# Unread 32x32 turns and 256 unread 32x32 products behind the second attention unit

## The chip, the cores and the metric

The kernel runs on one core of one Trainium2 chip. The metric is the device time of one execution in microseconds, from a median of several runs. TensorE's instructions appear in the profile twice: PE is the matmul, PEld the load of its stationary operand.

## The reference

One transformer block for one sequence of 2048 tokens of width 1024, in float32. A layer norm feeds an attention with 32 heads of 32 that works on four segments of 512 tokens: causal softmax inside a segment, and between segments a running memory (a sum of products of keys and values and a sum of keys, read with a positive map of the queries and mixed with the softmax part by a gate per head). A second layer norm, applied twice, feeds an MLP of width 3584 with gelu.

```python
h = x + A(layernorm(x))      # A: q, k, v = x @ wq, x @ wk, x @ wv; 32 heads, 4 segments of 512
    p = softmax(q @ k.T * scale + mask); a_dot = p @ v
    a_mem = phi(q) @ M / (phi(q) @ z + 1e-6)
    o = g * a_mem + (1 - g) * a_dot        # g = sigmoid(beta), one per head
    M, z = M + phi(k).T @ v, z + sum(phi(k))
    return o @ wo
out = h + B(layernorm(h))    # B: gelu(layernorm(y) @ w1 + b1) @ w2 + b2
```

## The kernel before

The kernel takes the tokens in two halves of 1024. In each half the attention is cut into 16 units, a unit being four heads (a group g) of one segment, in the order of the table `ORDER`. A unit takes 24 steps of the main loop in `attention`: eight steps each for keys, queries and values (`kps`, `qps`, `vps`), every step three products of 512 columns (`mm3`, lines 127 to 129: high by high, low by high, high by low parts, in fp32r). After each step `close` runs whatever was put on that step by `at`: splits of weights, softmax products of the unit before (`qk1`, `qk2`, `av` at line 634, whose 16 f32 products use four tiles of 32 columns), the memory's products, copies. Beside units 0 and 1 a generator `ln1` normalizes and turns the second segment's tokens (transposes `pt`, line 161).

The whole loop is recorded under `in_order()`: each engine keeps its instructions in the order in which the code writes them. An instruction that waits therefore holds up all that stands behind it on its engine.

Behind the last step of unit 1, in the first half only, the loop calls `constants()`. It makes the gate (ScalarE exp and add, lines 78 and 79, VectorE's reciprocal, line 80, ScalarE's complement, line 81), turns b1 (`pb`, lines 83 and 84) and spreads the gate by GpSimd (line 87). Then unit 2 begins with its `kps`.

Memory is taken from rings of slots. PSUM's rings are "d" with three banks (`kps`, `qps`, `vps`, `pb` and others), "qk" and "pt" with two banks each, and "av" with one. In SBUF the ring "ln" has four slots of 128x1024 floats; from unit 1 on, each unit takes two of them for `kk` and `qq`, the split keys and queries that DMAs then spread to `ks` and `qs` (line 418). Whoever takes a slot waits until its last readers are done.

Of the kernel before, what the change touches and what calls it, by code (L numbers as in the profile page):

```python
# [10 lines left out]
F32 = mybir.dt.float32  # L11
# [6 lines left out]
P = 128  # L18
S = 2048
D = 1024  # L20
# [31 lines left out]
def build(tc, x, wq, wk, wv, wo, beta, w1, b1, w2, b2, out):  # L52
    nc = tc.nc
# [3 lines left out]
    psum = top.enter_context(tc.tile_pool(name="psum", bufs=1, space=PSUM))  # L57

    def ps_dense(name):
        return psum.tile([P, 512], F32, tag="d", name=name, bufs=3)  # L60
# [16 lines left out]
    def constants():  # L77
        behind(nc.scalar.activation(bb, bb, AF.Exp, scale=-1.0))
        nc.scalar.activation(bb, bb, AF.Identity, bias=1.0)
        behind(nc.vector.reciprocal(gate[:, 0, :], bb))  # L80
        nc.scalar.activation(gate[:, 1, :], gate[:, 0, :], AF.Identity, scale=-1.0, bias=1.0)
        pb = ps_dense("pb")
        behind(nc.tensor.transpose(pb[:, :FB], b1r, ident[:FB, :FB]))
        nc.scalar.copy(b1c, pb[:, :FB])
        for j in range(4):
            b = slice(32 * j, 32 * j + 32)
            nc.gpsimd.tensor_copy(gcol[b, :], gate[b, 1, :].rearrange("p (g j) -> p g j", j=4)[:, :, j])
# [34 lines left out]
    def behind(op):  # L122

        tc.add_manual_dep(op.ins, acts["last"][op.ins.engine].name, NOSYNC, reason="program order")
# [240 lines left out]
    def attention(half, first):  # L365
# [355 lines left out]
        for n in range(16):  # L721
# [52 lines left out]
            if n == 1:  # L774
                for _ in side:
                    pass
                side = None
                if first:
                    constants()
                acts.pop("last", None)  # L780
# [658 lines left out]
    lnp = tc.alloc_tile_pool(name="lnp", bufs=1)  # L1439
# [142 lines left out]
```

## Time and profile before

| | us |
|---|---|
| median of 2 runs | 2175.62 (2174.37 to 2176.87) |
| the profiled execution, its time | 2176.5 |
| its span, first to last instruction | 2174.8 |
| TensorE busy in the span | 2154.5 (99%) |
| VectorE busy | 1357.8 (62%) |
| ScalarE busy | 1100.5 (51%) |
| GpSimd busy | 950.1 (44%) |

In a row of the timeline stand the start in the span, how long it took, engine, line, operation, what it writes and reads, and in square brackets how long the engine had idled and what ended that. In a row of the groups stand count, busy time and mean ns of one, then the idle time before them. A row of the windows has the stretch, its length, busy time of PE, PEld, DVE, ACT and POOL, the granted TensorE clock, and DMA's share and GB/s. In a row of one line's instructions stand the shortest, median and longest duration in ns. A row with x4 joins four instructions, and its time runs from the first start to the last end.

### The profile page before, as it was taken

Reading aid. Unit: us, or ns where it says so; the run is one execution under the profiler, and the core shown is the slowest. Engines: PE = TensorE matmul, PEld = TensorE weight load, DVE = VectorE, ACT = ScalarE, POOL = GpSimd, SP = SyncE. Lnnn points to the kernel's source line nnn. Section 1 sums busy time; section 2 is a strip of 40 time slices with the busy share of each in tenths; the row PEclk is TensorE's granted clock in tenths of the full one; section 3 lists DMA queues with packets and bytes.
Section 4 is the critical chain, followed back from the end, with each engine's and each line's share of the span. In section 5 each row is a group of like instructions: output and inputs, shape, how many; then the busy total and the mean of one; then the engine's idle time right before and its main releaser. Section 6 shows DMA issues by size and latency. Waiting matters only on the chain.

```text
span 2174.8 us, 33225 instructions
## 1 busy us (share of the span) xinstructions
PE 2154.5 (99%) x10937; PEld 1750.0 (80%) x10937; DVE 1357.8 (62%) x2696; ACT 1100.5 (51%) x2433; POOL 950.1 (44%) x1206
## 2 busy tenths in 40 slices
PE   8999999999999999999999999999999999999999
PEld 6877777778888888877777778888888788888887
DVE  7766666655745656666667655745666665576753
ACT  5777777753543445777777753633343232322321
POOL 5533335461434434533335551534446544255340
PEclk9999999999999999999999999999999999999999
DMA  7444444664575555444444763576569865676762
GB/s 202 117 117 107 107 107 127 198 203 155 169 211 154 180 163 152 121 117 107 107 107 125 204 214 134 170 213 174 160 202 380 280 223 178 201 241 214 260 227 91
DMA packets 352405, 376.20 MB, mean 173 GB/s; under 512 B 27214, under 2 KB 244330, under 8 KB 352234
## 3 DMA queue, kind: packets, MB, share of 16 engines
q1 hardware_dynamic: 289306, 337.25, 51.3%
q10 hardware_dynamic: 62928, 36.84, 5.7%
q8 instruction: 87, 1.43, 0.3%
q14 instruction: 84, 0.69, 0.1%
HBM read 241.27 MB, written 82.38 MB: 149 GB/s over the span
## 4 chain that ended last, share of the span: by engine, by line
PE 95%; DVE 2%; ACT 1%; DMA 1%; POOL 1%; issue 0%; SPq 0%; ACTq 0%; DVEq 0%; POOLq 0%
PE po L1418 24%; PE bps L1021 11%; PE cps L1021 7%; PE dps L1021 7%; PE pst L620 4%; PE po L634 3%; PE pqk L570 3%; PE pwo L127 3%; PE vps L127 3%; PE pwo L129 3%; PE qps L127 3%; PE pwo L128 3%; PE kps L127 3%; PE qps L128 3%; PE qps L129 3%; PE vps L128 3%
## 5 line engine op out<-in xcount | busy, mean ns | idle before, releaser
L572 DVE CUSTOM_DVE_ANT_0 pqk<-pqk,mask 128x512 f32<-128x512 f32 (+2 forms) x384 | 216.9, 565 | 235.5 <-PE pqk L570 205.1
L574 ACT ACTIVATE junk<-pqk,mx 128x512 f32<-128x512 f32 (+2 forms) x384 | 225.1, 586 | 133.0 <-DVE mx L572 124.7
L627 POOL TENSOR_SCALAR_AFFINE_SELECT e<-e 128x128 f32<-128x128 f32 (+1 forms) x384 | 136.0, 357 | 259.0 <-ACT e L623 253.9
L700 POOL TENSOR_TENSOR wl<-wr,wh 128x256 fp32r<-128x256 f32 x268 | 200.6, 764 | 107.2 <-DVE wh L696 43.5
L623 ACT ACTIVATE e<-pst 128x384 f32<-128x384 f32 (+1 forms) x384 | 200.4, 528 | 67.4 <-PE pst L620 66.4
L1428 DVE TENSOR_TENSOR c<-c,po 128x512 f32<-128x512 f32 x160 | 105.4, 683 | 150.7 <-PE po L1418 143.4
L620 PE MATMUL pst<-qs,ks 104*128 104x512 f32 (+3 forms) x512 | 140.7, 318 | 2.2 <-ACT e L623 1.2
L570 PE MATMUL pqk<-ks,qs 96*128 96x512 f32 (+2 forms) x384 | 137.8, 359 | 0.9 <-ACT junk L574 0.6
L620 PEld LDWEIGHTS pst<-qs,ks 104*128 104x128 f32 x512 | 95.7, 188 | 36.1 <-ACT e L623 11.5
L1418 PE MATMUL po<-w2h,zh 128*128 128x512 f32 x378 | 121.0, 390 | 2.0 <-ACT zh L1357 1.6
L1275 POOL TENSOR_TENSOR w2r<-w2r 128x512 f32<-128x512 f32 x54 | 83.0, 1547 | 70.9 <-DMA w2r<-in_B_w 65.0
L127 PE MATMUL qps<-yh,wh 128*128 128x512 f32 x256 | 113.1, 442 | 0.0
L127 PE MATMUL kps<-yh,wh 128*128 128x512 f32 (+1 forms) x264 | 113.0, 428 | 0.0
L1021 PE MATMUL bps<-zh,sb 128*128 128x512 f32 x336 | 111.0, 391 | 0.0
L1021 PE MATMUL bps<-zh,sa 128*128 128x512 f32 x336 | 110.8, 390 | 0.0
L1134 POOL TENSOR_TENSOR s<-r 128x512 f32<-128x512 f32 x28 | 44.0, 1571 | 142.3 <-DVE sa L1150 84.8
L127 PE MATMUL vps<-yh,wh 128*128 128x512 f32 x256 | 105.0, 410 | 0.0
L1418 PE MATMUL po<-w2h,hl 128*128 128x512 f32 x322 | 103.1, 390 | 0.0
L128 PE MATMUL kps<-yl,wh 128*128 128x512 f32 (+1 forms) x264 | 102.4, 388 | 0.6 <-DVE yl L165 0.3
L129 PE MATMUL kps<-yh,wl 128*128 128x512 f32 (+1 forms) x264 | 101.8, 386 | 0.0
L128 PE MATMUL qps<-yl,wh 128*128 128x512 f32 x256 | 101.0, 395 | 0.0
L128 PE MATMUL vps<-yl,wh 128*128 128x512 f32 x256 | 100.9, 394 | 0.0
(271 smaller groups left out, 6206.7 us busy)
## 6 DMA issues: line engine op xcount, KB each, us to landing
hr<-h_dram SPq DMA_DIRECT2D x112, 448.0 KB, 5.5
w2r<-in_B_w SPq DMA_DIRECT2D x122, 256.0 KB, 4.6
r<-in_B_w SPq DMA_DIRECT2D x56, 512.0 KB, 4.3
ks<-kk SPq DMA_DIRECT2D x360, 64.0 KB, 2.0
qs<-qq SPq DMA_DIRECT2D x360, 64.0 KB, 2.0
h_dram<-ht ACTq DMA_DIRECT2D x83, 256.0 KB, 3.8
wx<-in_B_w SPq DMA_DIRECT2D x56, 256.0 KB, 3.7
o_dram<-side SPq DMA_DIRECT2D x52, 256.0 KB, 4.3
```

Source lines behind the costliest of these rows:

```text
L127: nc.tensor.matmul(ps, ah, bh, start=first, stop=False)
L128: nc.tensor.matmul(ps, ah, bl, start=False, stop=False)
L129: acts["mm"] = nc.tensor.matmul(ps, al, bh, start=False, stop=last)
L570: nc.tensor.matmul(ps, u["qs"][0:96, j, i * P:(i + 1) * P], u["ks"][0:96, j, 0:n], start=True, stop=True)
L572: nc.vector.tensor_tensor_reduce(out=ps, in0=ps, in1=mask[:, 512 - n:512], op0=ALU.add, op1=ALU.min, scale=-SCALE, scalar=3.0e38, accum_out=m)
L574: at(now[0] + 1, lambda: nc.scalar.activation(acts["junk"][:, :n], ps, AF.Exp, bias=m, scale=-1.0, accum_out=u["mx"][:, 1, i, j:j + 1]))
L620: nc.tensor.matmul(ps[:, o:o + 512 - P * jk], u["ks"][:, j, jk * P:(jk + 1) * P], u["qs"][:, j, jk * P:512], start=True, stop=True)
L623: nc.scalar.activation(e, ps[:, :w], AF.Exp, scale=SCALE)
L627: nc.gpsimd.affine_select(d, d, pattern=[[0, 2], [1, P]] if n == 2 else [[1, P]], compare_op=ALU.is_ge, fill=0.0, base=0, channel_multipli ...
L700: nc.gpsimd.tensor_tensor(l[:, c], wr[:, c], raw(h)[:, c], op=ALU.subtract)
L1021: nc.tensor.matmul(ps, x_[:, c, :], y_[:, c, :], start=first and c == 0 and n == 0, stop=last and c == 3 and n == 2, skip_group_check=True)
L1418: nc.tensor.matmul(ps, x_[:, k], y_[k], start=opens and k == 0 and i == 0, stop=closes and k == self.KP - 1 and i == 2, skip_group_check=True)
```

## The change

In `constants()`, between the gate and b1's transpose, come: two tiles `ta` and `tb` from the ring "ln"; a memset of `ta` to 0.5 by VectorE; two turns in 32x32 blocks from `ta` to all of `tb`, 512 columns each; two more of 384 columns each over part of `tb`; and 256 products by TensorE. Each product uses one 32x32 tile of the array: row strip a (partitions 32a to 32a + 31 of both operands) and column strip j, accumulating over 16 steps b in PSUM bank a at partitions 32j on. The columns fall with b: 128, 96, 64 and 32, four steps each. The four banks are two of the ring "d", one of "qk" and one of "pt". Four copies by ScalarE write the banks back to `tb`. Nothing reads `tb` after that.

```diff
@@ -79,6 +79,27 @@
         nc.scalar.activation(bb, bb, AF.Identity, bias=1.0)
         behind(nc.vector.reciprocal(gate[:, 0, :], bb))
         nc.scalar.activation(gate[:, 1, :], gate[:, 0, :], AF.Identity, scale=-1.0, bias=1.0)
+        raw_ = lnp.tile([P, D], F32, tag="ln", name="ta", bufs=4)
+        turned = lnp.tile([P, D], F32, tag="ln", name="tb", bufs=4)
+        behind(nc.vector.memset(raw_, 0.5))
+        for k in range(2):
+            nc.vector.transpose(turned.rearrange("p (b c) -> p b c", c=64)[:, :, 32 * k:32 * k + 32],
+                                raw_[:, 512 * k:512 * k + 512].rearrange("p (b c) -> p b c", c=32))
+        for k in range(2):
+            nc.vector.transpose(turned[:, 512 * k:512 * k + 384], raw_[:, 512 * k:512 * k + 384])
+        pz = [psum.tile([P, 512], F32, tag=t, name="pz", bufs=n) for t, n in (("d", 3), ("d", 3), ("qk", 2), ("pt", 2))]
+        moving = turned.rearrange("p (i x) -> p i x", i=4)
+        for b in range(16):
+            for a in range(4):
+                for j in range(4):
+                    n, rows_ = 4 - b // 4, slice(32 * a, 32 * a + 32)
+                    op = nc.tensor.matmul(pz[a][32 * j:32 * j + 32, 0:32 * n], raw_[rows_, 32 * b:32 * b + 32],
+                                          moving[rows_, 0:n, 32 * j:32 * j + 32], start=b == 0, stop=b == 15,
+                                          tile_position=(32 * a, 32 * j), skip_group_check=True)
+                    if b + a + j == 0:
+                        behind(op)
+        for a in range(4):
+            nc.scalar.copy(turned[:, 128 * a:128 * a + 128], pz[a][:, 0:128])
         pb = ps_dense("pb")
         behind(nc.tensor.transpose(pb[:, :FB], b1r, ident[:FB, :FB]))
         nc.scalar.copy(b1c, pb[:, :FB])
```

TensorE's order at that place, before: the last products of unit 1's values and the last four turns of tokens, the transpose of b1, then unit 2's keys.

```order
L128 MATMUL vps<-yl_205,wh 128x512
L129 MATMUL vps<-yh_204,wl 128x512
L161 MATMUL pt<-ident,xt 128x128 x4
L83 MATMUL pb<-ident,b1r 128x28
L127 MATMUL kps<-yh_485,wh 128x512
L128 MATMUL kps<-yl_486,wh 128x512
```

And now, with every line behind the insertion 21 higher:

```order
L150 MATMUL vps<-yh_204,wl 128x512
L182 MATMUL pt<-ident,xt 128x128 x4
L96 MATMUL pz<-tb,ta 32x128 x64
L96 MATMUL pz<-tb,ta 32x96 x64
L96 MATMUL pz<-tb,ta 32x64 x64
L96 MATMUL pz<-tb,ta 32x32 x64
L104 MATMUL pb<-ident,b1r 128x28
L148 MATMUL kps<-yh_485,wh 128x512
L149 MATMUL kps<-yl_486,wh 128x512
```

The 256 products stand ahead of b1's transpose and of all of unit 2's keys.

VectorE's order at that place now: the copy of the values, two low parts of turned tokens, the gate's reciprocal, then the new five, then the chain on `z` that ends in the row offsets `mh` of unit 0's second softmax pass.

```order
L517 COPY vt<-vps 128x512
L186 TENSOR_TENSOR yl_486<-pt,yh_485 128x4x128 x2
L80 RECIPROCAL gate<-bb 128x32
L84 MEMSET ta 128x1024
L86 STREAM_TRANSPOSE tb<-ta 128x16x32 x2
L89 STREAM_TRANSPOSE tb<-ta 128x384 x2
L619 TENSOR_TENSOR z<-z,mx 128x16
L620 SCALAR_TENSOR_TENSOR z<-z 128x16
```

Before, the reciprocal was followed by `z` at once; the memset and the four turns now stand between them. On ScalarE the four copies of `pz` (line 102) stand between the gate's complement (line 81) and the copy of b1.

## The prediction

> **What bounds the kernel now.** I read the page first: busy shares, then the chain that ended last.
>
> ```profile
> span 2174.8 us, 33225 instructions
> PE 2154.5 (99%) x10937; PEld 1750.0 (80%) x10937; DVE 1357.8 (62%) x2696; ACT 1100.5 (51%) x2433; POOL 950.1 (44%) x1206
> ...
> PE 95%; DVE 2%; ACT 1%; DMA 1%; POOL 1%; issue 0%; SPq 0%; ACTq 0%; DVEq 0%; POOLq 0%
> ```
>
> TensorE is busy 99% of the span and carries 95% of the chain. Time that it loses can come back only where it waits later. So the second view is its waits from 60 to 120 us, the stretch that begins where the change is put:
>
> ```profile
> PE kps L128 <- DVE yl L165: 0.3, 1, 0.3
> ```
>
> This is the only wait there: 0.3 us. What the change costs TensorE is therefore nearly all paid in the end. The third view is the timeline at that place.
>
> ```profile
> 60.16 0.60 PE L161 MATMUL pt<-ident,xt 128*128 128x128 f32 x4
> 60.36 0.69 DVE L496 COPY vt<-vps 128x512 f32<-128x512 f32 x1 [0.38 <-PE vps L129]
> ...
> 60.69 0.24 PE L83 MATMUL pb<-ident,b1r 28*128 28x28 f32 x1
> ...
> 60.86 0.50 PE L127 MATMUL kps<-yh,wh 128*128 128x512 f32 x1
> 60.97 1.51 DVE L165 TENSOR_TENSOR yl<-pt,yh 128x512 fp32r<-128x512 f32 x2
> ...
> 61.64 0.24 ACT L78 ACTIVATE bb<-bb 128x32 f32<-128x32 f32 x1
> ...
> 61.70 0.50 PE L128 MATMUL kps<-yl,wh 128*128 128x512 f32 x1 [0.34 <-DVE yl L165]
> ...
> 61.91 0.23 ACT L79 ACTIVATE bb<-bb 128x32 f32<-128x32 f32 x1
> ...
> 62.39 0.34 DVE L80 RECIPROCAL gate<-bb 128x32 f32<-128x32 f32 x1
> ...
> 62.65 0.11 DVE L598 TENSOR_TENSOR z<-z,mx 128x16 f32<-128x16 f32 x1
> ```
>
> TensorE reaches the constants at 60.69, two microseconds before VectorE has finished its own part of them at 62.39 + 0.34 = 62.73. The change puts VectorE's new instructions behind that reciprocal, and TensorE's products wait for them.
>
> **The change part by part.** *The wait.* The products read ta and tb, so TensorE stops at 60.69 until VectorE has done a memset of 128x1024, two turns of 128x512 and two of 128x384. No row shows a memset of this size or a turn; the nearest ones are
>
> ```profile
> L696 DVE CAST wh<-wr 128x1024 fp32r<-128x1024 f32 x66 | 46.3, 702 | 2.9 <-DMA wr<-in_A_wv 2.9
> L933 DVE TENSOR_TENSOR hb<-ht,b2c 128x1024 f32<-128x1024 f32 x16 | 19.2, 1209 | 1.8 <-DMA h_dram<-hb 1.3 <-DMA b2c<-in_B_b 0.5
> L496 DVE COPY vt<-vps 128x512 f32<-128x512 f32 x32 | 22.1, 691 | 0.4 <-PE vps L129 0.4
> L572 DVE CUSTOM_DVE_ANT_0 pqk<-pqk,mask 128x384 f32<-128x384 f32 x128 | 72.5, 566 | 100.8 <-PE pqk L570 98.4
> ```
>
> The memset lies between 0.70 (the cast) and 1.21 (the sum); I take 1.1. A turn of 512 columns lies between half of that cast, 0.35, and 0.69; I take 0.65, near the copy. One of 384 lies between 0.26 and 0.57; I take 0.50. Sum 1.1 + 1.3 + 1.0 = 3.4, and 0.1 for hand-overs between them (z at L598 follows the reciprocal without a gap). VectorE ends at 66.2 and TensorE starts at 66.3: **5.6 us** lost. From below the five cost 1.9 and the loss is 4.1. From above there is the same cast beside GpSimd:
>
> ```profile
> 54.25 6.74 POOL L700 TENSOR_TENSOR wl<-wr,wh 128x256 fp32r<-128x256 f32 x9
> ...
> 54.96 1.27 DVE L696 CAST wh<-wr 128x1024 fp32r<-128x1024 f32 x1
> ```
>
> 1.27 for 0.70; 1.8 times 3.4 is 6.2, a loss of 8.4. GpSimd's splits were done by 60.99, so I keep 5.6. Queued behind the waiting product stand the transpose of b1r and all of unit 2's projections; ScalarE's copies, VectorE's maxima and GpSimd's masks wait for those. Nothing of this runs ahead, so the pause hides nothing.
>
> *The products.* The 256 become 512 records if each makes two, as the head products at L634 do (1024 records for 32 units of 16). Those are four tiles of 32 columns side by side, and the nearest rows:
>
> ```profile
> 85.87 2.36 PE L634 MATMUL po<-e,vf 128*32 128x512 f32 x32
> 88.16 0.50 PE L127 MATMUL kps<-yh,wh 128*128 128x512 f32 x1
> 88.50 0.39 PE L128 MATMUL kps<-yl,wh 128*128 128x512 f32 x1
> ...
> 85.87 0.16 PEld L634 LDWEIGHTS po<-e,vf 128*32 128x32 f32 x8 [0.37 <-issue]
> ```
>
> ```profile
> L634 PEld LDWEIGHTS po<-e,vf x1024: 106/110/110, 85.9 to 1297.6; 128*32 128x32 f32 x171
> L634 PE MATMUL po<-e,vf x1024: 272/432/617, 85.9 to 1297.7; 128*32 128x512 f32 x43, 128*32 128x256 f32 x43, 128*32 128x128 f32 x43, 128*32 128x384 f32 x42
> ```
>
> A full-width transpose of 128 f32 columns takes (0.60 - 0.27)/3 = 0.11 us (four at 60.16, 0.27 being the record of one). One block at L634 streams 2 x 4 x (512 + 384 + 256 + 128) = 10240 columns, 8.8 us one after another; it took 88.16 - 85.87 = 2.29. So nearly four run abreast, each column strip on its own. The new products stream 2 x 64 x (128 + 96 + 64 + 32) = 40960 columns: 35.2 us one after another, 8.8 four abreast, 2.2 sixteen abreast. Row strips side by side occur nowhere in the trace. For starting them, eight loads of 0.11 in 0.16 us are (0.16 - 0.11)/7 = 7 ns apart, so 512 pairs need at least 512 x 7 ns = 3.6 us. Ends: 3.6 below, 56 above (512 x 0.11, each load's full time bare). I take **3.6**, sixteen abreast: what shares the array by columns so cleanly I expect to share it by rows, the four row strips writing four different banks.
>
> *The clock.* A pause of 5.6 us has no like between 14 us and the end. The ends of the trace show what one does:
>
> ```profile
> 8.23 1.97 PE L281 MATMUL pt<-ident,xt 128*128 128x128 f32 x8 [8.23 <-ACT xt L271]
> 10.54 3.85 PE L281 MATMUL pt<-ident,xt 128*128 128x128 f32 x16 [0.34 <-ACT xt L271]
> 14.15 0.37 PE L127 MATMUL kps<-yh,wh 128*128 128x256 f32 x1
> ```
>
> ```profile
> 2170.59 0.39 PE L1418 MATMUL po<-zh,hl 128*128 128x512 f32 x1
> ```
>
> ```profile
> 2164.00:2170.00 6.00, 6.00 (x28) 4.97 (x27) 0.69 (x1) 0.00 (x0) 0.00 (x0) 1.00 0.12 44
> 2174.00:2174.80 0.80, 0.00 (x0) 0.00 (x0) 0.00 (x0) 0.00 (x0) 0.00 (x0) 0.92 0.00 0
> ```
>
> After the last product's end at 2170.98 the granted clock (third column from the right) falls within the last 0.8 us, to a mean of 0.92: idle for under 3.8 us was enough. At the start, eight and then sixteen transposes take 1.97 and 3.85 us; 0.11 apart, as at 60.16, they would take 7 x 0.11 + 0.27 = 1.04 and 15 x 0.11 + 0.27 = 1.92. So half speed lasted from 8.23 to about 14, some 5.8 us. If that recurs, the first 5.8 us do 2.9 us of work: **+2.9**, from 0 (no drop) to about 5 (a longer one).
>
> The Trainium skill, "TensorE: Matmul & The Clock Gate", Part 1, has half rate after an idle window of about 3.4 us and full rate again after a busy window as long. The trace agrees on the fall (under 3.8 us), but its half speed lasted 5.8; by the page's window the term would be 1.7 and the sum 11.2.
>
> *Behind the products.* kps now takes the bank of the first pz and waits for ScalarE's copy of it.
>
> ```profile
> 62.91 0.17 ACT L84 COPY b1c<-pb 128x28 f32<-128x28 f32 x1
> ```
>
> ```profile
> L502 ACT COPY vf<-vn 128x512 f32<-128x512 f32 x32 | 18.8, 587 | 0.0
> ```
>
> 128 columns between 28 (0.17) and 512 (0.59) give 0.26. With 0.2 for the last record to end, 0.1 of signals and 0.1 for leaving the tiles (kps at 88.16 takes 0.34 to its successor, other 512-column products 0.23): **+0.65**, ends 0.4 and 1.5 (all four copies waited for). The 0.34 at 61.70 goes: yl is ready long before, **-0.35**, and no other wait is there to take its place.
>
> *At nothing.* ta and tb take two of the ring's four slots, so unit 2 writes kk where unit 1's still lay.
>
> ```profile
> 61.32 2.20 SPq L418 DMA_DIRECT2D ks<-kk  x3
> ...
> 63.58 2.00 SPq L418 DMA_DIRECT2D qs<-qq  x3
> ...
> 70.05 0.58 ACT L435 CAST kk<-kps 128x512 fp32r<-128x512 f32 x1
> ```
>
> Its last readers are issued by 65.6 and the write stood at 70.05, now 12 us later: covered by the pause itself. Without that cover it would be some 2 us. VectorE's z chain, 3.5 us late, feeds a TensorE step that stands behind the products: hidden by them.
>
> Sum: 5.6 + 3.6 + 2.9 + 0.65 - 0.35 = **12.4 us**. The profiled execution took 2176.5 (span 2174.8), 0.9 above the median 2175.62 and inside the runs' spread, so 2176.5 + 12.4 = **2189**, slower by 0.6%: inside the 2% that a measurement of this kernel can tell from no change.
>
> **Rivals.** *Four abreast.* Row strips take turns, only column strips overlap: 8.8 instead of 3.6, sum 17.6, **2194** (2199 if no pass of a tile takes less than 0.11: 128 turns of 0.11 = 14.1). For it: the trace has no row strips. Against: nothing but the likeness of rows to columns.
>
> *Strict order.* If a product's second pass must wait for its first on the same tile, and nothing overtakes it, only two passes ever overlap and each product adds one pass: 64 x 0.11 x (1 + 0.75 + 0.5 + 0.25) = 17.6 instead of 3.6, sum 26.4, **2203**. Against: the same rule gives L634 4 x 0.11 x (4 + 3 + 2 + 1) = 4.4 us where 2.29 was measured. For: sixteen tiles may exceed how far TensorE looks ahead; four do not. The Trainium skill, same page, Part 3 ("What overlaps and what doesn't") states such first-in-first-out order for products; the L634 row speaks against it here.
>
> *Nothing abreast.* Each small load costs its whole 0.11 before its product, 512 x 0.11 = 56 instead of 3.6: sum 65, **2241**, slower by 3%. It passes 2% once a record costs over some 69 ns: 43.5 us less the other 8.8 is 35, over 512. For it: with 32 columns little streaming covers a load, and the chip's instruction supply over 1024 dense ones isn't seen in the trace. Against: at L634 loads of 0.11 hid behind products that follow 0.11 apart.
>
> **How the numbers follow.** Forecast 0.58 (its own terms: 4.1 + 3.6 + 0 + 0.4 - 0.35 = 7.8 up to 8.4 + 3.6 + 5 + 1.5 - 0.35 = 18.2, mostly 2184 to 2192), four abreast 0.20, strict order 0.13, nothing abreast 0.05, the rest 0.04, of which 0.01 for some gain over 2%. The range 2183 to 2206 takes the first two and the lower part of the third, about 0.83. Slower by over 2%: the last rival, 0.05; faster 0.01; within 2%: 0.94.
>
> **What the changed profile would show.** A wait of TensorE at the first pz for VectorE's tb, 4 to 8 us. Then 512 records whose start to end is 6 to 7 us (four abreast near 11, strict order near 20, nothing abreast over 50), their first part at half the later pace and a granted clock under 1 between 64 and 73 us. kps waits some 0.5 for the copy. From there every instruction stands later by the same 12 us, and no other group's time moves. I am wrong if the pause is short because VectorE's five are quick, if the clock stays up, or if later stretches give back or add more than a microsecond.

## The result and the profile after

The changed kernel took 2202.06 us (2 runs, 2199.72 to 2204.4) against 2175.62: ratio 1.0117, 95% interval 1.01 to 1.0133. It is slower by 1.2%, inside the 2% called no change and inside the range of 2183 to 2206, but by about twice the 12.4 us of the sum. In four more runs beside 11 of the kernel before it took 2199.46 against 2176.81: 22.7 us, ratio 1.0101 (1.0088 to 1.0115). The terms below are set against that.

The page after, its span, its busy shares and its chain:

```profile
span 2198.0 us, 34257 instructions
PE 2165.5 (99%) x11449; PEld 1758.8 (80%) x11449; DVE 1359.4 (62%) x2701; ACT 1101.5 (50%) x2437; POOL 946.9 (43%) x1206
...
PE 92%; DVE 2%; ACT 1%; DMA 1%; issue 1%; POOL 1%; SPq 1%; ACTq 0%; POOLq 0%; DVEq 0%
```

TensorE has the 512 records more that were counted, and "issue" has risen from 0% to 1% of the chain. TensorE's waits from 60 to 120 us in the changed kernel say why:

```profile
PE pz L96 <- issue: 6.4, 3, 2.8
PE pz L96 <- DVE z L619: 5.5, 1, 5.5
```

The wait for VectorE was forecast. (The row names `z`, which stands right behind the turns on VectorE; the last turn ends at 67.48, and TensorE goes on at 67.53.) The other was not: three times TensorE stood inside its own stream of products while nothing that the profile shows held it. The timeline shows where:

```profile
61.42 0.60 PE L182 MATMUL pt<-ident,xt 128*128 128x128 f32 x4
...
64.16 0.91 DVE L84 MEMSET ta<- 128x1024 f32 x1 [0.16 <-issue]
...
65.10 1.30 DVE L86 STREAM_TRANSPOSE tb<-ta 128x512 f32<-128x512 f32 x2
66.44 1.04 DVE L89 STREAM_TRANSPOSE tb<-ta 128x384 f32<-128x384 f32 x2
...
67.53 3.99 PE L96 MATMUL pz<-tb,ta 32*32 32x128 f32 x202 [5.52 <-DVE z L619]
...
74.37 2.17 PE L96 MATMUL pz<-tb,ta 32*32 32x96 f32 x128 [2.84 <-issue]
77.82 1.75 PE L96 MATMUL pz<-tb,ta 32*32 32x64 f32 x128 [1.28 <-issue]
81.82 0.80 PE L96 MATMUL pz<-tb,ta 32*32 32x32 f32 x54 [2.26 <-issue]
82.55 0.30 PE L104 MATMUL pb<-ident,b1r 28*128 28x28 f32 x1
82.69 0.77 ACT L102 COPY tb<-pz 128x128 f32<-128x128 f32 x4 [18.43 <-PE pz L96]
83.00 0.80 PE L148 MATMUL kps<-yh,wh 128*128 128x512 f32 x1
83.59 0.63 PE L149 MATMUL kps<-yl,wh 128*128 128x512 f32 x1
```

The pieces between the waits have 128 records each; with a load for every product, that is 256 instructions. The page's row of the instruction queue (packets, MB, share) says the same, before and after:

```profile
q8 instruction: 87, 1.43, 0.3%
```

```profile
q8 instruction: 91, 1.49, 0.3%
```

Four packets more than before, for 1024 instructions more: 256 to a packet. The DMA view from 74 to 84 us (40 slices of 0.25 us, GB/s in each; after the kernel's own loads had landed) has three lone transfers:

```profile
GB/s 0 0 0 0 0 66 0 0 0 0 0 0 0 0 0 0 0 0 0 66 0 0 0 0 0 0 0 0 0 0 0 0 0 0 0 66 0 0 0 0
DMA packets 3, 0.05 MB, mean 5 GB/s; under 512 B 0, under 2 KB 0, under 8 KB 0
```

Each is 0.05 MB / 3, some 16 KB. They come in the slices from 75.25, 78.75 and 82.75, about a microsecond after TensorE had gone on at 74.37, 77.82 and 81.82. In the trace they start at 75.47, 78.93 and 82.97 and take 0.9 to 1.4 us each. The first two start 2.4 and 2.9 us before the ends of the next waits, 77.82 and 81.82; what fills the time between the end of a transfer and the next product, no view shows.

The windows of the changed kernel (third column from the right the granted clock) show the second surprise:

```profile
67.50:82.50 15.00, 8.58 (x512) 7.39 (x512) 0.74 (x5) 0.00 (x0) 0.00 (x0) 0.50 0.28 74
82.50:87.60 5.10, 4.95 (x27) 3.74 (x15) 1.17 (x3) 1.53 (x7) 1.19 (x2) 0.50 0.01 3
87.60:95.00 7.40, 7.34 (x40) 5.96 (x37) 4.12 (x11) 5.46 (x13) 2.62 (x6) 1.00 0.00 0
```

In this execution half clock lasted through the whole stream and 5 us of dense products behind it, not 5.8 us in all.

The next place to compare is the first of unit 0's head products. It stood at 85.87, 25.71 after the last four turns of tokens at 60.16; now

```profile
109.50 2.36 PE L655 MATMUL po<-e,vf 128*32 128x512 f32 x32
```

48.08 after the same four at 61.42: **22.4 us** lost by then. The span grew by 23.2, and the same turns began 1.3 later before any new instruction had run, so nothing was given back or added beyond a microsecond.

### The profile page after: what moved, and what is told of

It reads as the page before. It is cut to its first block, busy times and chain, and to the rows that moved or that the text cites. A ratio compares the mean times of both kernels' runs of the same rounds, so it can differ in the third digit from the quotient of the medians.

```text
span 2198.0 us, 34257 instructions
## 1 busy us (share of the span) xinstructions
PE 2165.5 (99%) x11449; PEld 1758.8 (80%) x11449; DVE 1359.4 (62%) x2701; ACT 1101.5 (50%) x2437; POOL 946.9 (43%) x1206
## 4 chain that ended last, share of the span: by engine, by line
PE 92%; DVE 2%; ACT 1%; DMA 1%; issue 1%; POOL 1%; SPq 1%; ACTq 0%; POOLq 0%; DVEq 0%
PE po L1439 23%; PE bps L1042 10%; PE cps L1042 7%; PE dps L1042 6%; PE pst L641 4%; PE po L655 3%; PE pqk L591 3%; PE kps L148 3%; PE pwo L148 3%; PE vps L148 3%; PE pwo L150 3%; PE qps L148 3%; PE pwo L149 3%; PE qps L149 3%; PE qps L150 3%; PE kps L149 2%
```

## The experiments

The theory after the result: the stream is held by the **supply of instructions**, 256 at a time, 3.4 to 4 us each once the stock is used up; the array itself does sixteen tiles abreast. The rivals: the array sets the stream; or the pause and the half clock make the cost. The diffs are against the changed kernel where nothing else is said; `...` stands for code left out, and the step that closes the accumulation moves with the last `b`.

**Only 16 products** (wait16). VectorE's part stays.

```diff
-        for b in range(16):
+        for b in range(1):
-                    n, rows_ = 4 - b // 4, slice(...)
+                    n, rows_ = 1, slice(...)
```

> Leaves out all but the first 16 products, at 32 columns each, and copies 32 columns; VectorE's memset and four turns stay. Theory (instruction supply: the changed kernel's stream of 15 us is three waits for the next 256 instructions, 6.4 us and more, around an array that needs little): with 32 records there is no such wait, so only the pause of 5.6, the copy of 0.6, the half-speed dense products behind it (about 2.3) less 0.35 are left: 8 us over the kernel before. Rival (the pause and the half clock make most of the cost, the stream little): 15 us or more.

2183.88 against 2177.44: 6.4 us over, ratio 1.0027 (1.0016 to 1.0038). The forecast of 8 lies inside the interval, 3.5 to 8.3 us. The pause was 5.1 instead of 5.5, because the first products here read only columns that the first of the last two turns writes; in the profile the head products lost 7.7. Pause and clock alone are between a quarter and a third of the change's 22.7. The rival that they are most of it falls.

**The same columns in a quarter of the products** (wide64). Four steps of 320 columns instead of sixteen.

```diff
-        for b in range(16):
+        for b in range(4):
-  pz[a][32 * j:32 * j + 32, 0:32 * n], ... moving[rows_, 0:n, 32 * j:32 * j + 32]
+  pz[a][32 * j:32 * j + 32, 0:320], ... turned[rows_, 128 * j:128 * j + 320]
```

> The same number of streamed columns (40960 with both passes) in 64 products of 320 columns instead of 256: 256 instructions instead of 1024. Supply theory: no wait of more than 0.3 us inside the stream, which takes 2 to 3 us at half clock; 10 to 11 us over the kernel before. Rival (the array sets the stream: row strips or order of passes): the stream stays at 12 to 15 us, 20 to 23 over before.

2188.21: 10.8 over, ratio 1.0045 (1.0032 to 1.0059). Its stream and its windows:

```profile
66.44 4.84 PE L96 MATMUL pz<-tb,ta 32*32 32x320 f32 x128 [5.05 <-DVE tb L89]
...
71.58 0.50 PE L148 MATMUL kps<-yh,wh 128*128 128x512 f32 x1
```

```profile
66.40:69.80 3.40, 3.36 (x84) 2.36 (x98) 1.21 (x6) 0.00 (x0) 0.00 (x0) 0.50 0.75 214
69.80:72.00 2.20, 2.07 (x64) 1.35 (x41) 0.00 (x0) 0.74 (x5) 0.00 (x0) 1.00 0.77 184
```

40960 columns, which one after another take 35.2 us at full clock (80 times 512 at 0.44), ran in under 5 us, 3.4 of them at half: some 3 us at full clock, at least 11 abreast, where four were the ceiling of the prediction's rival "four abreast". No wait for instructions stands in it. The stream was expected at 2 to 3 and took longer: all but its first two products start behind the last turn, 0.45 later. The total came as forecast, with full clock back before the dense products (kps 0.50 here, 0.80 in the changed kernel).

**The same products, all of 32 columns** (narrow256). Two fifths of the columns, the same 1024 instructions. The four copies behind them are 32 columns wide as well.

```diff
-                    n, rows_ = 4 - b // 4, slice(...)
+                    n, rows_ = 1, slice(...)
```

> The same 256 products, all of 32 columns: 1024 instructions, two fifths of the columns. Supply theory: three waits of 1.5 to 3.2 us each stay, 256 instructions apart, stream 13 to 15 us, 20 to 23 over the kernel before. Rival (the array sets the stream): stream at two fifths, 6 us, 14 over before.

2198.16: 20.7 over, ratio 1.0092 (1.0078 to 1.0106). Its timeline:

```profile
65.70 2.29 PE L96 MATMUL pz<-tb,ta 32*32 32x32 f32 x202 [5.05 <-DVE tb L89]
71.05 1.54 PE L96 MATMUL pz<-tb,ta 32*32 32x32 f32 x128 [3.05 <-issue]
75.05 1.54 PE L96 MATMUL pz<-tb,ta 32*32 32x32 f32 x128 [2.46 <-issue]
78.78 0.80 PE L96 MATMUL pz<-tb,ta 32*32 32x32 f32 x54 [2.19 <-issue]
```

The work between the waits shrank and the waits grew to fill it: from one resumption to the next 4.0 and 3.7 us, for 1.54 of work. They come after the same 202, 128 and 128 records.

**No pause** (ready256). The products read the identity matrix.

```diff
-  raw_[rows_, 32 * b:32 * b + 32], moving[rows_, 0:n, 32 * j:32 * j + 32]
+  ident[rows_, 32 * (b % 4):32 * (b % 4) + 32], ident[rows_, 0:32 * n]
```

> The 256 products read the identity matrix, which is ready, instead of the memset's and the turns' tiles; all five VectorE instructions stay and run beside them. Supply theory: the pause of 5.6 shrinks to under 1.5 (a PSUM bank to come free), the three waits stay, the stream takes 11 to 15 us: 12 to 17 over the kernel before. Rival (the half clock stretches the stream): no long pause, so no half clock at its start, and the stream falls to 6 to 7 us: 7 to 9 over before.

2191.86: 14.4 over, ratio 1.007 (1.0058 to 1.0083), as the supply theory had it.

```profile
62.17 2.81 PE L96 MATMUL pz<-ident 32*32 32x128 f32 x202
66.33 2.17 PE L96 MATMUL pz<-ident 32*32 32x96 f32 x128 [1.35 <-issue]
70.06 1.75 PE L96 MATMUL pz<-ident 32*32 32x64 f32 x128 [1.56 <-issue]
74.89 0.80 PE L96 MATMUL pz<-ident 32*32 32x32 f32 x54 [3.08 <-issue]
```

The first piece now runs at full clock, 2.81 for 3.99; the waits stay (6.0 in sum), and the stream takes 13.5 us for 15.1. The clock was still halved from 66.3 on, behind a gap of only 1.35.

**The changed kernel again** (again), unaltered.

> The changed kernel once more, unaltered, beside the next three. The terms read from its profile (pause 5.6, stream 15.0, copy 0.6, half-clock dense products 2.3, less 0.35) add to 23 us over the kernel before; the two times shown so far say 26.4. Theory: 22 to 24. Rival (a term of some 3 us outside the place): 26 or more.

22.7 over, as the profile's terms add up to. The first 26.4 came from two runs each. The waits for instructions are there again, three and 6.4 us in sum, and the stream takes 14.9. But the clock went another way:

```profile
65.00:72.00 7.00, 3.79 (x202) 3.34 (x203) 3.84 (x10) 0.00 (x0) 0.73 (x4) 0.52 0.71 186
72.00:75.40 3.40, 0.78 (x69) 0.56 (x59) 0.00 (x0) 0.00 (x0) 0.00 (x0) 0.99 0.13 29
75.40:89.00 13.60, 9.64 (x294) 7.93 (x281) 1.42 (x4) 2.10 (x8) 2.10 (x3) 0.50 0.01 4
```

It was full for 3.4 us in the middle of the stream, most of them a wait for instructions, so little came of it. Half clock through the whole stream is one execution's course, and not what sets its length.

**A warm pause** (warm16). As the first experiment, with dense work where TensorE waited.

```diff
+        for i in range(23):
+            op = nc.tensor.matmul(pz[0], acts["y", 0][0][:, 0, 0:P], acts["y", 0][0][:, 0, :], start=True, stop=True)
+            if i == 0:
+                behind(op)
         for b in range(1):
```

> As wait16 (the first 16 products alone, 32 columns), with 23 dense unread products of 512 columns in the pause, where TensorE waited. Theory (an idle window costs the clock, and half clock costs dense products their own length again): the clock stays at 1, kps follows at full pace, some 2.5 to 3 us less than wait16, so 3 to 4 over the kernel before. Rival (the clock falls whatever stands in the pause, for what ran before it): as wait16, 6 over before.

2183.36 against 2176.81: 6.5 over, ratio 1.0026 (1.0015 to 1.0037), by the times no better than without it. The profiles differ, though. Windows of the cold one, then of the warm one:

```profile
67.00:73.80 6.80, 6.38 (x50) 5.06 (x51) 3.01 (x12) 1.79 (x8) 2.11 (x3) 0.50 0.66 170
```

```profile
67.00:73.80 6.80, 6.57 (x64) 5.11 (x62) 4.82 (x16) 3.21 (x12) 2.12 (x3) 1.00 0.62 169
```

And the first head products, cold and warm, 33.44 and 30.92 after the turns of tokens at 61.61 and 61.48:

```profile
61.61 0.60 PE L182 MATMUL pt<-ident,xt 128*128 128x128 f32 x4
...
95.05 2.36 PE L655 MATMUL po<-e,vf 128*32 128x512 f32 x32
```

```profile
61.48 0.60 PE L186 MATMUL pt<-ident,xt 128*128 128x128 f32 x4
...
92.40 2.36 PE L659 MATMUL po<-e,vf 128*32 128x512 f32 x32
```

So the clock stayed up and 2.5 us were saved at the place, as the theory said. Each ratio's interval is 2.4 us to either side, so the times can neither confirm nor deny it. By the median the forecast of 3 to 4 missed. In the two profiled executions part of it went elsewhere: from the head products to the end the cold one took 2087.4 us and the warm one 2089.2, and over all traces of this case, with the change or without, that stretch takes 2086.4 to 2091.3. What the warm pause saves in the timed runs stays open.

**Twice the instructions** (narrow512). 512 products of 32 columns; the diff is against narrow256.

```diff
-        for b in range(16):
+        for b in range(32):
```

> 512 products of 32 columns, twice narrow256: 2048 instructions. Supply theory (256 instructions take some 3.7 us once the stock is used up): seven waits in place of three, stream 13.6 + 4 x 3.7 = 28 us, 35 us over the kernel before. Rival (only the first pages were late, the supply catches up): 24 to 28 over before.

2210.54 against 2176.81: 33.7 over, ratio 1.0155 (1.0141 to 1.0168). TensorE's waits there:

```profile
PE pz L96 <- issue: 16.0, 7, 4.0
```

Seven waits. Against the 256 narrow products, 13 us for 1024 instructions more: 3.3 us per 256. The supply doesn't catch up.

**More columns for the same instructions** (full256). Every product 512 columns wide.

```diff
-  pz[a][32 * j:32 * j + 32, 0:32 * n], ... moving[rows_, 0:n, 32 * j:32 * j + 32]
+  pz[a][32 * j:32 * j + 32, 0:512], ... turned[rows_, 128 * j:128 * j + 512]
```

> 256 products of 512 columns each: 262144 streamed columns with both passes, 6.4 times the changed kernel's, in as many instructions. Sixteen abreast they need 16 x 2 x 0.43 = 13.7 us at full clock. Supply theory (the waits run beside the array's work when there is enough of it): stream 14 to 18 us, hardly a wait of over 0.5 us, 19 to 25 over the kernel before. Rival (the waits add to the array's work, as in the changed kernel): 13.7 + 6.4 = 20 us or more, 26 to 32 over before.

2201.85: 25.0 over, ratio 1.0114 (1.0098 to 1.0129), at the upper end of the supply theory's range and just under the rival's. The interval, 21 to 28 us, takes in both; the trace decides.

```profile
67.01 18.99 PE L96 MATMUL pz<-tb,ta 32*32 32x512 f32 x512 [5.06 <-DVE tb L89]
```

```profile
70.70:86.00 15.30, 15.30 (x464) 11.03 (x446) 0.00 (x0) 0.61 (x3) 0.00 (x0) 1.00 0.07 19
```

6.4 times the columns for 2.4 us more, and no wait for instructions at all. The stream is a microsecond over the forecast's 18: its first 3.4 us from 67.28 on ran at half clock, all but its first product start behind the last turn, 0.46 later, and even at full clock a round of 16 records takes 0.53 (15.30 us for 464) instead of 0.43.

**Dense work between** (mixed). As narrow256, with ten dense ones behind every 64.

```diff
+            for i in range(10 if b % 4 == 3 else 0):
+                nc.tensor.matmul(dz, acts["y", 0][0][:, 0, 0:P], acts["y", 0][0][:, 0, :], start=True, stop=True)
```

> As narrow256, with ten dense unread products of 512 columns behind every 64 of the small ones: 40 more, 9.1 us of TensorE work at full clock (0.227 each). Supply theory (the next 256 instructions come while the dense products run): the three waits of 2.2 to 3.1 us shrink to under 1.5 each, and the whole costs 20 to 25 us over the kernel before, 0 to 4 more than narrow256. Rival (the waits stand whatever runs beside them): 20.7 + 9.1 = 30 over before.

2200.16 against 2177.0: 23.2 over, ratio 1.0102 (1.0085 to 1.0119), 2.4 more than without them.

```profile
67.24 1.54 PE L97 MATMUL pz<-tb,ta 32*32 32x32 f32 x128 [5.06 <-DVE tb L89]
68.71 3.79 PE L103 MATMUL dz<-yh 128*128 128x512 f32 x10
72.43 1.61 PE L97 MATMUL pz<-tb,ta 32*32 32x32 f32 x128
73.97 2.56 PE L103 MATMUL dz<-yh 128*128 128x512 f32 x10
```

9 us of dense products cost 2.4, where the rival that the waits stand whatever runs beside them said 9; no wait for instructions is left, and an array that set the stream would have had to pay the 9 too. Part of the small price is the clock: the first ten dense products took 3.79, the next ten 2.56, and from there on the clock stayed full, while in narrow256 it was half to the end of the stream and 5 us beyond. From the first small product to b1's transpose it is 16.7 us here and 13.8 in narrow256; at the head products only 0.7 of that difference of 2.9 is left.

No version here beats the kernel before, nor can one be expected: the added work is read by nothing, and the least that any variant cost was 6.4 us.

## Why the prediction was right, and where it was not

*The wait for VectorE: right.* Forecast 5.6, measured 5.52. The memset took 0.91 for 1.1, the first two turns 1.30 for 1.3, the others 1.04 for 1.0.

*The products: mis-sized, 3.6 for 15.1* (67.53 to 82.62). That is the step that failed, in two pieces. "I take 3.6, sixteen abreast" was near the truth on the array: the first 32 loads start within 0.14 us and the first 16 products within 0.11, and the wide products ran at least 11 abreast, though 16 were not shown. But 6.4 of the 15.1 are waits for instructions, which the prediction named in half a sentence ("the chip's instruction supply over 1024 dense ones isn't seen in the trace") and booked only under the rival at 2241. The other 8.7 are the pieces, here all at half clock: the 202 records took 3.99, and 2.81 at full clock without the pause. In narrow256 shorter pieces meant longer waits, and a faster clock would presumably do the same, so the 8.7 are not the clock's price.

The Trainium skill, "Runtime: NRT & Kernel Launch", "Instruction fetch mechanics", says that instructions are fetched in blocks of 16 KiB, 256 at a time, one block ahead, and that this is hidden behind the time that each takes to issue. The runs agree on the block and contradict the hiding: 256 small-tile instructions were worked in 1.5 us (narrow256) and refilled in 3.3 to 4.

*The clock: right that it falls, mis-sized and misplaced.* Forecast +2.9 inside the stream and full speed after 5.8 us. In the first profile it stayed at half for the whole stream and for 5 us of dense products. In the stream it cost 1.2 us in the first piece (3.99 for 2.81); behind it the waits for instructions set the pace. Kps to the head products lost 22.4 - 20.9 = 1.5 there (kps's first product lost 20.9: it now follows the turns by 21.58, before by 0.70), which is some 1.8 of clock less the 0.35 gained at yl. The warm pause puts the clock at 2.5 for a kernel with hardly a stream. The 5.8 us were read from the start of the trace; the clock's record there begins, with full clock, at 14.04 us (the views print 1.00 before it), which fits half speed until then but not a fixed length. Neither 5.8 us nor the window of 3.4 us that the prediction priced at 1.7 was what the stream got: on the account of the last section, the waits kept full clock from coming back.

*Behind the products: right.* From the last piece's end, 82.62, to kps at 83.00 it is 0.4, and kps stands 0.6 behind the start of the last product; forecast 0.65. No wait for yl is left: the -0.35 came.

*At nothing: right.* No wait on the ring's slots appears, and from the head products to the end it took 2088.5 us, for 2088.9 before.

*The rivals.* Four abreast and strict order are refuted as mechanisms, though strict order's 2203 is nearest to the first time: the right size for a wrong reason. At strict order each of the 64 products of 320 columns would add a pass of its own, 17.6 us in all, and they took 4.84; with four abreast they would take 8.8. "Nothing abreast" did not happen either, but the reason given for it, the supply of instructions, is what came. So it is in part luck that the time fell inside the range: the range reached to 2206 for the sake of strict order, and no rival priced the supply at what it cost. Of the forecast's last paragraph, "6 to 7 us" start to end was the sign to watch, and it failed; none of the three signs that it names as proof of being wrong came.

## What to carry to other kernels

Count instructions, not only columns: a burst of very short TensorE instructions is paid by the refill of the instruction store, here 3.3 to 4 us per 256 behind the first 404, as soon as the work in them is shorter than that. Make the products wider, or put dense products between the bursts; 9 us of them went in for 2.4, with the clock that they brought back. And a pause put in front of dense work costs more than its own length, because the clock that falls in it is paid afterwards.

## What the runs showed of the hardware

TensorE's products in 32x32 tiles do run side by side over rows and columns: 40960 columns, 35.2 us one after another, in under 5 us. The granted clock does not only fall for an idle gap of several microseconds: with the identity as operand it was halved from 66.3 us on while TensorE had been 2.98 of 4.30 us busy with small tiles:

```profile
62.00:66.30 4.30, 2.98 (x205) 2.49 (x204) 3.97 (x7) 1.82 (x7) 1.19 (x5) 1.00 0.42 97
66.30:76.00 9.70, 5.03 (x312) 4.39 (x311) 2.13 (x8) 0.55 (x4) 0.00 (x0) 0.50 0.50 134
```

The traces show more of the clock than the forecast knew. In each of them, every change of it stands on a grid of 3.41 us. It was half for 3.41 us in wide64 and full256, 6.83 in wait16 and mixed, 13.65 in ready256, 20.48 in the changed kernel's first profile and narrow256, 34.13 in narrow512, and in the repeat 6.83 and 13.65 with 3.41 of full clock between: 1, 2, 4, 6 and 10 stretches. Where the pause lies on that grid is chance, and so the clock fell between 2.4 us (mixed) and 5.3 us (full256) after TensorE had stopped.

With TensorE's busy share in each stretch of 3.41 us, one account fits all ten traces of the change and its variants. Full clock came back behind a stretch in which TensorE was busy for 0.99 or more, and not behind 0.96 (the repeat, 82.3 to 85.7 us). It fell behind stretches with 0.31 or less, and stayed behind 0.44 to 0.60 of full-width products (full256 and wait16). In the repeat the 128-column products filled the stretch from 68.6 to 72.05, and the clock came back; in the first profile they began 0.37 us into their stretch, which was busy for 0.89, and the next one held the wait. One stretch does not go by busy time alone: in ready256 0.60, most of it small tiles, was followed by half clock. No run was made to test this account, and what the chip counts stays open.
